# Experts of 64 tokens or fewer get slots, weight buffers and a short branch of their own between the turns of the others

## Chip, cores and metric

The kernel runs on one core of a Trainium2 chip. The metric is the device time of one execution in microseconds (us); lower is better. The program is one launch that does the whole computation.

## The reference

Three layers follow one another: gated linear attention, a dense layer with three-way maximum, and a mixture of eight experts of which each token uses one. The change touches the last layer only:

```python
N, D, E, F = (3072, 384, 8, 1024)          # tokens, model width, experts, hidden width
logits = x @ w_gate
e_idx = np.argmax(logits, axis=1)
...
for e in range(E):
    mask = e_idx == e
    if not mask.any():
        continue
    h = np.maximum(x[mask] @ w1[e], 0.0)
    ye = h @ w2[e]
    out[mask] = gate_w[mask, None] * eom[mask, e, None] * ye
```

Everything is float32. How many tokens go to which expert depends on the data. For the inputs of this kernel the routing gives experts 0 to 7 these numbers of tokens: 4, 281, 1078, 7, 47, 262, 107 and 1286. So three experts (0, 3 and 4) have 64 tokens or fewer.

## The kernel before

**Stages.** Attention and the dense layer run over eight blocks of 384 tokens. While the last block is finished, the expert layer starts. From then on the core works through *units*: a unit is up to 256 tokens of one expert (or up to 320 in the last unit of an expert, so that a rest of 64 or fewer rides along). The unit list is computed on the chip from the routing (`units_a_ops` to `units_e`, L730 to L835, all on VectorE): which expert each unit has, whether its expert is new (`meta`), and its kind (`kinds`). The kinds are 0 (two tiles of 128 tokens), 1 (an expert with 64 tokens or fewer, "alone"), 2 (two tiles and a third of 64) and 3 (one tile). Here there are 15 units: 0 to 4 are expert 7, 5 is expert 0 (alone), 6 is expert 1 (kind 2), 7 to 10 expert 2 (the last of kind 2), 11 and 12 experts 3 and 4 (alone), 13 expert 5 (kind 2), 14 expert 6 (kind 3). Units 0 and 1 run within the end of the dense layer; units 2 to 14 are the *turns* of the function `turn` (L1279), unrolled in the program. From unit 10 on, a turn lies within an If on the number of units.

**One turn** of unit u, in program order: registers and token gathers for unit u+2 (GpSimd, indirect DMA, L857); the first four pieces of the second weight matrix are split into a high and a low float32r part if the expert is new (`fresh`, `split2`, ScalarE and VectorE, L644 and L645); `up` (L918: for each of eight slices of the hidden layer 15 matmuls, then one ScalarE and one or two VectorE evictions out of one of three PSUM banks, L919 and L922); the other four pieces; the load of the first weight matrix of unit u+2; `tx` (transposes of the gathered tokens of unit u+1, L880, and their split) and `split1` of unit u+1 if it is new; `down` (L961 and L966/L967, one PSUM bank for each tile, evicted by ScalarE into a fresh output tile, L973, and scattered to HBM by GpSimd, L938); the load of the second weight matrix of unit u+2. Each engine runs its instructions in this order, and waits only where its next instruction needs something.

**Weights.** Each expert has 1.57 MB in each of two matrices. They are loaded into the raw buffers `s1` and `s2`, two of each, by the parity of the unit (`stage`, L847, on SP's queue, two units ahead). Kinds 0, 2 and 3 split them into `w1H`, `w1L`, `w2H`, `w2L`; kind 1 multiplies with the raw float32 buffers.

**An alone unit** runs through the same turn with short arms: `tx` copies the transposed tokens to `xF` (L891), `up` has six float32 products of 64 tokens in pairs over the two halves of the array (L909, 12 instructions in the trace) and one ScalarE copy to `hF` (L932), `down` transposes the hidden values (L985), applies the maximum with zero (L988, L990), has eight float32 products (L909, 16 instructions) and adds the two halves up (`put_sum`, L948 to L950). Only the experts' own numbers decide which arm a turn takes: `by_kind` (L895) is a chain of Ifs on a register.

**The list before the turns.** The steps that end the dense layer and start the experts are written out by hand (`then`, L1215 on): `units_b` makes the slot of each token and two big products for the index lists (`mark`, L668 to L670), `up_some(1, ...)` is the up stage of unit 1, `units_c` looks the indices up (`lookup`), then `units_d`, `units_e`, and the gathers of units 2 and 3.

## Time and profile before

| what | value |
|---|---|
| median of 3 runs | 763.56 us (763.53 to 764.07) |
| profiled execution, device time | 759.59 us |
| its span, first to last instruction | 757.8 us |
| TensorE matmuls busy | 705.9 us (93% of the span) |
| VectorE, ScalarE, GpSimd busy | 52%, 38%, 17% |
| mean granted TensorE clock | 0.978 of 2.4 GHz |

Times are counted from the span's start. "Idle before" is time in which an engine did nothing before an instruction, and the arrow says what ended it: another engine's instruction, a DMA, or "issue" where the profile shows nothing that it waited for. PEld is TensorE's weight load, which runs beside the matmuls; a name with a q behind it (PEldq, ACTq) is an engine's sequencer with its branches and register loads. A granted clock of 1.00 is 2.4 GHz, 0.5 is 1.2 GHz.

### The profile page before, as it was taken

The page shows a single profiled execution, that of the slowest core. Times are in us where ns is not written, and L with a number is a line of the kernel's source. Part 1 is how long each engine was busy: PE and PEld are TensorE (multiplying, and loading weights), DVE is VectorE, ACT ScalarE, POOL GpSimd, SP SyncE. Part 2 cuts the span into 40 slices and gives each one's busy share as a digit, 9 for nine tenths or more (in the row PEclk, how much of TensorE's full clock was granted, in tenths as well). Part 3 has the DMA queues.
Part 4 walks back from the last instruction along what each step waited for, and adds up shares of the span by engine and source line. Part 5 has one row for each costly group of instructions (what it writes and reads, how often), then busy time and mean ns, then how long its engine had stood idle before and what let it go on. Part 6 is the DMA issues. An engine that isn't in the chain of part 4 may idle for free. (4 is left out here: it accounts for less than half of the span.)

```text
span 757.8 us, 14282 instructions
## 1 busy us (share of the span) xinstructions
PE 705.9 (93%) x5056; PEld 656.3 (87%) x5056; DVE 397.7 (52%) x929; ACT 288.5 (38%) x752; POOL 126.8 (17%) x136
## 2 busy tenths in 40 slices
PE   8999999999899999999999999999989999977980
PEld 8989999798799999999999999999949899954970
DVE  7968976477957547364143566532237422213640
ACT  4455344454444424335131243332236423224540
POOL 1000000011121202111111130422232322231220
PEclk9999999999999999999999999999989999997995
DMA  9823400651412215000000060214553113666310
GB/s 265 340 57 137 144 1 22 181 134 45 124 51 73 69 40 131 15 24 5 22 19 10 22 229 22 62 58 138 208 214 112 52 51 132 204 237 218 99 43 17
DMA packets 23407, 76.33 MB, mean 101 GB/s; under 512 B 8026, under 2 KB 12132, under 8 KB 20208
## 3 DMA queue, kind: packets, MB, share of 16 engines
q1 hardware_dynamic: 17424, 60.95, 24.6%
q0 software_dynamic: 4704, 12.91, 5.4%
q8 instruction: 67, 1.10, 0.6%
q10 hardware_dynamic: 1152, 0.89, 0.4%
q14 instruction: 60, 0.49, 0.2%
HBM read 89.26 MB, written 9.94 MB: 131 GB/s over the span
## 5 line engine op out<-in xcount | busy, mean ns | idle before, releaser
L918 PE MATMUL psM<-cx,w1H 128*128 128x256 f32 (+1 forms) x576 | 112.1, 292 | 5.3 <-DVE ch L922 4.9
L482 POOL TENSOR_TENSOR hL<-hm,hH 128x384 fp32r<-128x384 f32 x36 | 42.2, 1172 | 396.6 <-ACT hH L477 396.6
L456 PE MATMUL hps<-xH,wH 128*128 128x384 f32 x432 | 103.9, 347 | 1.4 <-ACT xH L367 1.3
L456 PE MATMUL hps<-xH,wL 128*128 128x384 f32 x432 | 98.4, 335 | 1.6 <-DVE wL L425 1.6
L918 PEld LDWEIGHTS psM<-cx,w1H 128*128 128x128 f32 x576 | 91.3, 188 | 8.8 <-DVE ch L922 4.3
L456 PE MATMUL hps<-xL,wH 128*128 128x384 f32 x432 | 98.6, 335 | 0.0
L961 PE MATMUL psP<-w2H,ch 128*128 128x384 f32 x368 | 96.8, 338 | 1.1 <-ACT w2H L644 1.1
L922 DVE SCALAR_TENSOR_TENSOR ch<-psM,ch 128x256 fp32r<-128x256 f32 (+1 forms) x128 | 43.9, 371 | 95.2 <-ACT ch L919 92.1
L918 PE MATMUL psM<-cx,w1L 128*128 128x256 f32 (+1 forms) x288 | 83.6, 290 | 0.0
L456 PEld LDWEIGHTS hps<-xH,wH 128*128 128x128 f32 x432 | 74.1, 188 | 7.4 <-ACT xH L367 2.1
L456 PEld LDWEIGHTS hps<-xH,wL 128*128 128x128 f32 x432 | 76.9, 188 | 2.3 <-DVE wL L425 2.3
L456 PEld LDWEIGHTS hps<-xL,wH 128*128 128x128 f32 x432 | 77.3, 188 | 0.2 <-DVE xL L368 0.2
L492 PE MATMUL ops<-wo,hH 128*128 128x400 f32 x258 | 68.5, 346 | 0.2
L961 PEld LDWEIGHTS psP<-w2H,ch 128*128 128x128 f32 x368 | 66.6, 188 | 2.0 <-issue 1.3
L463 DVE TENSOR_TENSOR hm<-hm,hps 128x384 f32<-128x384 f32 x48 | 26.4, 551 | 69.7 <-PE hps L456 62.7
L919 ACT ACTIVATE ch<-psM 128x256 fp32r<-128x256 f32 (+1 forms) x96 | 37.7, 402 | 64.8 <-PE psM L918 55.4
L938 POOL DMA_INDIRECT out<-yo,sidx x30 | 31.1, 1038 | 185.8 <-ACT yo L973 147.8
L961 PE MATMUL psP<-w2L,ch 128*128 128x384 f32 x184 | 61.5, 334 | 0.0
L857 POOL DMA_INDIRECT xg<-x2d,gidx x49 | 50.4, 1029 | 30.1 <-PE psM L918 12.2
L918 PEld LDWEIGHTS psM<-cx,w1L 128*128 128x128 f32 x288 | 54.2, 188 | 0.0
L477 ACT CAST hH<-hm 128x384 fp32r<-128x384 f32 x43 | 22.0, 513 | 81.0 <-DVE hm L466 77.2
L492 PEld LDWEIGHTS ops<-wo,hH 128*128 128x128 f32 x258 | 47.0, 188 | 1.3 <-ACT hH L477 0.5
(238 smaller groups left out, 1111.5 us busy)
## 6 DMA issues: line engine op xcount, KB each, us to landing
s1a<-in_ew SPq DMA_DIRECT2D x9, 1536.0 KB
s2a<-in_ew SPq DMA_DIRECT2D x9, 1536.0 KB
s1b<-in_ew SPq DMA_DIRECT2D x7, 1536.0 KB
s2b<-in_ew SPq DMA_DIRECT2D x7, 1536.0 KB
ws<-in_w SPq DMA_DIRECT2D x6, 1152.0 KB
at<-in_al SPq DMA_DIRECT2D x16, 336.9 KB
vt<-in_v SPq DMA_DIRECT2D x8, 576.0 KB
x2d<-xs SPq DMA_DIRECT2D x24, 192.0 KB
```

What stands on the lines that cost most here:

```text
L456: mm(ps, slab(a, f)[:, w, k], b[i][:, k], start=(n == 0), stop=(n == 8))
L463: nc.vector.tensor_max(m, m, ps)
L477: nc.scalar.copy(hH[i, f], m)
L482: (nc.gpsimd if not general and i > 1 else nc.vector).tensor_sub(hL[i, f], hps["m"], hH[i, f].bitcast(F32))
L492: mm(ps[:, :DM + NG], a[i, f][:, ts_], wo[f // 3][:, b, f % 3], start=(f + n == 0), stop=(f + n == 7))
L857: nc.gpsimd.indirect_dma_start(out=xg[u % 2, t][:p], out_offset=None, in_=x2d[:n, :], in_offset=bass.IndirectOffsetOnAxis(ap=gidx[:p, 3 * ...
L918: mm(ps, w[:, k, f * 128:(f + 1) * 128], x[:, k, :n], start=(k + m == 0), stop=(k + m == 4))
L919: nc.scalar.activation(chid(0, f, slice(0, n)), ps, AF.Relu)
L922: nc.vector.scalar_tensor_tensor(C["h"][f // 4][:, f % 4, to:to + b - a], ps[:, a:b], 0.0, chid(0, f, slice(a, b)).bitcast(F32), op0=ALU.m ...
L938: nc.gpsimd.indirect_dma_start(out=out[:, :], out_offset=bass.IndirectOffsetOnAxis(ap=sidx[:p, c:c + 1], axis=0), in_=y[:p], in_offset=Non ...
L961: mm(ps[:, :DM], chid(x, f, slice(128 * t, 128 * t + 128)), w[:, f], start=(f + n == 0), stop=(f == NE - 1 and n == 2))
```

## The change

An expert with a rest of 64 tokens or fewer and nothing else no longer gets a unit (`nu` subtracts `few`). It gets one of eight slots behind the unit slots in the index lists (62 instead of 54 columns), computed in `units_a_ops` and `units_b`, and the new `units_f` writes a list of these experts and their number to `tiny`. Kind 1 and its arms go.

Each of the turns 2 to 9 (i = 0 to 7) now has, behind `down`, an If on the number of such experts (`n_own > i`) with the function `own(i)`: the float32 arm of before, with its up products in two halves of 256 columns. Its tokens are gathered by `gather_own` into `xO`, transposed and copied to `xF` within the `tx` of the same turn (`own=True`: these three transposes run in all eight turns, whether there is such an expert or not). With the data above, `own` runs in turns 2, 3 and 4, all of expert 7, and the unit list has 12 entries: 0 to 4 expert 7, 5 expert 1, 6 to 9 expert 2, 10 expert 5, 11 expert 6.

The second pair of raw weight buffers now belongs to `own` (`stage_own`, loaded as soon as the one before is done); the units share one pair, so `stage(u + 1, 0)` comes at the start of turn u and `stage(u + 1, 1)` behind the pieces of `split2`. Of these pieces two instead of four come ahead of `up`. The output tiles are three fixed buffers, cleared once on GpSimd, and the scatters (`put`) come last in a turn, behind `own`, `gather_own` and, from unit 9 on, inside the arms of the If that holds the next turn. `put2` scatters units 0 and 1.

```diff
--- before.py
+++ after.py
-NS = 3 * (NU - NF)
+NS = 3 * (NU - NF) + NE
...
     def split2(j, pieces=range(NE)):
         for f in pieces:
-            split(*(t[:, f] for t in (C["s2"][j % 2], *C["w2"])))
+            split(*(t[:, f] for t in (C["s2"][0], *C["w2"])))
...
         nu = wt([128, NE], "nsl")
-        nc.vector.scalar_tensor_tensor(nu, q, 1.0, f, op0=ALU.add, op1=ALU.subtract)
+        nc.vector.scalar_tensor_tensor(nu, q, 1.0, few, op0=ALU.add, op1=ALU.subtract)
...
+
+        own = rtmp["own"] = wt([128, NE], "own")
+        nc.vector.tensor_sub(own, few, f)
+        yield
+        nth = rtmp["nth"] = wt([128, NE], "nth")
+        nc.vector.tensor_tensor_scan(nth, one8, own, 0.0, ALU.mult, ALU.add)
+        yield
         over = rtmp["over"] = q
         nc.vector.tensor_scalar(over, q, 3.0, 1.0, op0=ALU.mult, op1=ALU.add)
         yield
-        nc.vector.tensor_mul(over, over, f)
+        off = rtmp["off"] = wt([128, NE], "off")
+        nc.vector.tensor_sub(off, nth, over)
+        yield
+        nc.vector.tensor_sub(off, off, base)
+        yield
+        nc.vector.scalar_tensor_tensor(off, off, 3.0 * NU, own, op0=ALU.add, op1=ALU.mult)
+        yield
+        nc.vector.tensor_sub(off, off, f)
+        yield
+        nc.vector.tensor_mul(over, over, few)
         yield
...
     def units_b():
         bt = wt([128, NT, NE], "bt", BF16)
         sums = []
-        for n, name in (("over", "so"), ("base", "sl")):
+        for n, name in (("over", "so"), ("off", "sd"), ("base", "sl")):
             nc.vector.tensor_tensor(bt, oh, rtmp[n].unsqueeze(1).to_broadcast([128, NT, NE]), ALU.mult)
             sums.append(wt([128, NT], name))
             nc.vector.tensor_reduce(sums[-1], bt, op=ALU.add, axis=AX.X)
-        so, sl = sums
+        so, sd, sl = sums
         nc.vector.scalar_tensor_tensor(so, rdiv, 1.0, so, op0=ALU.add, op1=ALU.is_equal)
+        nc.vector.tensor_mul(so, so, sd)
         nc.vector.tensor_add(sl, sl, rdiv)
-        nc.vector.tensor_sub(sl, sl, so)
+        nc.vector.tensor_add(sl, sl, so)
         rtmp["q"] = mark(sl, ioS, NT)
...
-        nc.vector.tensor_copy(kinds[:, :NU], kd)
-
-        nc.vector.scalar_tensor_tensor(kinds[:, 2 * NU:], kd, 1.0, meta[:, NU:2 * NU], op0=ALU.is_equal, op1=ALU.max)
-        nc.vector.scalar_tensor_tensor(kinds[:, NU:2 * NU], kd, 1.0, meta[:, NU:2 * NU], op0=ALU.not_equal, op1=ALU.mult)
+        nc.vector.tensor_copy(kinds, kd)
+
+    def units_f():
+
+        own, nth = rtmp["own"], rtmp["nth"]
+        nc.vector.tensor_mul(own, own, nth)
+        wide = [128, NE, NE]
+        le = wt(wide, "bt")
+        nc.vector.tensor_tensor(le, own.unsqueeze(1).to_broadcast(wide), ioU[:, 1:NE + 1].unsqueeze(2).to_broadcast(wide),
+                                ALU.is_equal)
+        nc.vector.tensor_tensor(le, le, ioU[:, :NE].unsqueeze(1).to_broadcast(wide), ALU.mult)
+        ex = wt([128, NE], "fv")
+        nc.vector.tensor_reduce(ex, le, op=ALU.add, axis=AX.X)
+        nc.vector.tensor_copy(tiny[:, :NE], ex)
+        nc.vector.tensor_copy(tiny[:, NE:], nth[:, NE - 1:])
...
-        chg[u] = nc.values_load(kinds[0:1, 2 * NU + u:2 * NU + u + 1], engines=(ET.SP,), min_val=0, max_val=1)
+        chg[u] = nc.values_load(meta[0:1, NU + u:NU + u + 1], engines=(ET.SP, ET.Activation, ET.DVE), min_val=0, max_val=1)
-        new[u] = nc.values_load(kinds[0:1, NU + u:NU + u + 1], engines=(ET.Activation, ET.DVE),
-                                min_val=0, max_val=1)
+
+    def load(e, buf, n, cond):
+        s, w = (("s1", ew1), ("s2", ew2))[n]
+        nc.sync.dma_start(out=C[s][buf], in_=w[ds(e, 1)].rearrange("o p a b -> p (o a) b"), cond=cond)
 
     def stage(u, n):
-        s, w = (("s1", ew1), ("s2", ew2))[n]
-        nc.sync.dma_start(out=C[s][u % 2], in_=w[ds(eos[u], 1)].rearrange("o p a b -> p (o a) b"), cond=(chg[u] == 1))
+        load(eos[u], 0, n, chg[u] == 1)
+
+    def stage_own(i, both=range(2)):
+        if i < NE:
+            e = nc.values_load(tiny[0:1, i:i + 1], engines=(ET.SP,), min_val=0, max_val=NE - 1)
+            for n in both:
+                load(e, 1, n, n_own > i)
 
...
+    def take(x, p, c, n=NTOK):
+        nc.gpsimd.indirect_dma_start(out=x[:p], out_offset=None, in_=x2d[:n, :],
+                                     in_offset=bass.IndirectOffsetOnAxis(ap=gidx[:p, c:c + 1], axis=0),
+                                     bounds_check=n - 1, oob_is_err=False)
...
+    def gather_own(i):
+        if i < NE:
+            take(C["xO"], LAST, 3 * NU + i)
 
 
     def hidden():
+        C["y"] = [bp.tile([128, DM], F32, tag="hL", name="yo", bufs=7) for _ in range(3)]
+        for y in C["y"]:
+            nc.gpsimd.memset(y, 0.0)
...
-        def alone():
-            nc.scalar.copy(C["xF"], ps[0][:, :DM])
-
-        by_kind(u, {1: alone}, whole)
+                nc.tensor.transpose(ps[t][:, k * p:k * p + p], x[:p, k * 128:(k + 1) * 128], ident[:p, :p])
+        if own:
+            x = C["xO"]
+            nc.vector.tensor_copy(C["gO"], x[:LAST, DM:XW])
+            for k in range(3):
+                nc.tensor.transpose(ps[2][:, (3 + k) * LAST:(4 + k) * LAST], x[:LAST, k * 128:(k + 1) * 128], ident[:LAST, :LAST])
+        for t in range(tiles):
+            p = WIDTH[t]
+            x = ps[t][:, :3 * p].rearrange("p (k c) -> p k c", k=3)
+            h = hi[:, :, 128 * t:128 * t + p]
+            nc.scalar.copy(h, x)
+            nc.vector.tensor_sub(lo[:, :, 128 * t:128 * t + p], x, h.bitcast(F32))
+        if own:
+            nc.scalar.copy(C["xF"], ps[2][:, 3 * LAST:6 * LAST])
...
     def up(u):
-        def alone():
-            ps = bank(psM, "M", "psM1")
-            w = C["s1"][u % 2]
...
-
-        by_kind(u, {1: alone, 2: lambda: up_some(u, 256 + LAST, range(NE))}, lambda: up_some(u, 256, range(NE)))
-
-    def put(u, t, y, p):
-        c = 3 * u + t
+        by_kind(u, {2: lambda: up_some(u, 256 + LAST, range(NE))}, lambda: up_some(u, 256, range(NE)))
...
+    def send(y, p, c):
...
+    def put(u):
+        def some(*ts):
+            for t in ts:
+                send(C["y"][t], WIDTH[t], 3 * u + t)
+
+        some(0)
+        by_kind(u, {2: lambda: some(1, 2), 3: lambda: None}, lambda: some(1))
+
...
         if t == 2:
-            return put_sum(u, t, ps)
-        y = out_tile()
-        nc.scalar.activation(y, ps[:, :DM], AF.Copy, scale=gate[u % 2][:, t:t + 1])
-        if not general:
-            put(u, t, y, 128)
-        return y
+            return sum_up(C["y"][t], gate[u % 2][:64, t:t + 1], ps)
+        nc.scalar.activation(C["y"][t], ps[:, :DM], AF.Copy, scale=gate[u % 2][:, t:t + 1])
 
     def down(u):
-        def alone():
...
-        def tiles(n):
-            return lambda: [down_tile(u, t) for t in range(n)]
-
-        by_kind(u, {1: alone, 2: tiles(3), 3: tiles(1)}, tiles(2))
+        down_tile(u, 0)
+        by_kind(u, {2: lambda: [down_tile(u, t) for t in (1, 2)], 3: lambda: None}, lambda: down_tile(u, 1))
+
+
+
+    def own(i):
+        h, w = C["hF"], C["s1"][1]
+        for a in range(0, 512, 256):
+            ps = bank(psM, "M", "psM1")
+            for k in range(3):
+                x = C["xF"][:, k * LAST:(k + 1) * LAST]
+                halves(ps, 256, (x, x), [w[:, k, g * 512 + a:g * 512 + a + 256] for g in range(2)], k == 0, k == 2)
+            nc.scalar.copy(h[:, a:a + 256], ps[:, :256])
...
+        ps = bank(psO, "O", "psP")
+        w = C["s2"][1]
+        for f in range(4):
+            x = h[:, 512 + f * 128:512 + (f + 1) * 128]
+            halves(ps, DM, (x[:, :64], x[:, 64:]), (w[:, f], w[:, f + 4]), f == 0, f == 3)
+        sum_up(C["yO"], C["gO"], ps)
+        send(C["yO"], LAST, 3 * NU + i)
...
+    def put2(u):
+        for t in range(2):
+            send(C["y"][t], 128, 3 * u + t)
...
+    then(put2, 0)
     then(units_b)
...
     then(units_e)
+    then(units_f)
     then(gather, NF + 1)
...
-    for u in (NF, NF + 1):
-        load_meta(u)
-        for n in range(2):
-            stage(u, n)
-    C["xF"] = bp.tile([128, DM], F32, tag="hH", name="xF", bufs=7)
+    C["xO"], C["gO"] = bp.tile([128, XW], F32, tag="x32", name="xO"), wk.tile([LAST, 1], F32, name="gO")
+    C["xF"] = bp.tile([128, 3 * LAST], F32, tag="hH", name="xF", bufs=7)
     C["hF"] = bp.tile([128, FF2], F32, tag="x32", name="hF")
+    C["yO"] = bp.tile([128, DM], F32, tag="hH", name="yO", bufs=7)
     n_all = nc.values_load(meta[0:1, 2 * NU:2 * NU + 1], min_val=0, max_val=NU)
+    n_own = nc.values_load(tiny[0:1, NE:NE + 1], min_val=0, max_val=NE)
+    load_meta(NF)
+    for n in range(2):
+        stage(NF, n)
+    stage_own(0)
...
     def fresh(u, split, *a):
-        with tc.If(new[u] == 1):
+        with tc.If(chg[u] == 1):
...
+    gather_own(0)
     tx(NF)
...
     def turn(u):
         more = u + 1 < NU
-        ahead = u + 2 < NU
-        if ahead:
+        i = u - NF
+        if more:
+            stage(u + 1, 0)
+        if u + 2 < NU:
             load_meta(u + 2)
             gather(u + 2)
-        fresh(u, split2, low)
+        fresh(u, split2, range(2))
         up(u)
-        fresh(u, split2, high)
-        if ahead:
-            stage(u + 2, 0)
+        fresh(u, split2, range(2, NE))
         if more:
+            stage(u + 1, 1)
             with guard(u + 1):
-                tx(u + 1)
+                tx(u + 1, own=i < NE)
                 fresh(u + 1, split1)
         down(u)
-        if ahead:
-            stage(u + 2, 1)
-        if more and u + 1 >= NV:
-            with guard(u + 1):
+        if i < NE:
+            with tc.If(n_own > i):
+                own(i)
+            stage_own(i + 1)
+            gather_own(i + 1)
+        if u + 1 < NV:
+            put(u)
+        elif more:
+            with tc.If(n_all > u + 1) as c:
+                put(u)
                 turn(u + 1)
-
+            with c.Else():
+                put(u)
+        else:
+            put(u)
...
+    put2(1)
 
     for u in range(NF, NV):
         turn(u)
```

## Rows read from the trace of the kernel before

**Rows 1.** Busy time of each engine by window, one window for each turn; the last is the tail.

```profile
core 0: us, PE busy (x) PEld busy (x) DVE busy (x) ACT busy (x) POOL busy (x), PEclk, DMA share, GB/s
...
553.65:567.34 13.69, 9.93 (x43) 3.79 (x42) 6.11 (x14) 6.11 (x13) 4.92 (x4) 0.76 0.74 279
567.34:591.34 24.00, 23.29 (x148) 22.49 (x146) 13.60 (x37) 13.01 (x29) 6.65 (x6) 1.00 0.29 98
...
611.36:629.41 18.05, 18.05 (x130) 17.81 (x130) 4.95 (x14) 5.33 (x13) 5.04 (x5) 1.00 0.17 52
...
647.43:670.37 22.94, 22.94 (x146) 22.12 (x145) 4.72 (x19) 5.72 (x12) 6.05 (x6) 1.00 0.54 182
670.37:683.14 12.77, 7.37 (x42) 3.18 (x42) 2.07 (x7) 3.55 (x7) 4.86 (x5) 1.00 0.94 345
683.14:697.97 14.83, 11.41 (x41) 4.66 (x41) 5.53 (x12) 5.06 (x11) 2.96 (x3) 0.65 0.59 216
697.97:722.49 24.52, 23.36 (x147) 22.26 (x146) 13.69 (x37) 13.27 (x30) 6.26 (x6) 1.00 0.33 104
722.49:738.12 15.63, 13.42 (x96) 12.72 (x96) 7.64 (x17) 7.14 (x18) 3.94 (x4) 1.00 0.19 42
738.12:757.80 19.68, 0.00 (x1) 0.00 (x0) 0.00 (x0) 0.58 (x1) 1.03 (x1) 0.59 0.07 17
```

**Rows 2.** Timeline of TensorE in turns 11 and 12 (start, us, what, idle before).

```profile
670.37 2.79 PE L909 MATMUL psM<-s1b,xF 128*64 128x512 f32 x12
...
674.87 0.63 PE L985 MATMUL psH<-ident,hF 128*128 128x128 f32 x4 [0.56 <-ACTq L1272]
...
675.84 2.80 PE L909 MATMUL psP<-s2b,hF 128*64 128x384 f32 x16 [0.34 <-ACT hF L990]
683.14 4.49 PE L909 MATMUL psM<-s1a,xF 128*64 128x512 f32 x12 [4.50 <-issue]
```

**Rows 3.** Timeline of TensorE in turn 5.

```profile
559.17 0.67 PE L985 MATMUL psH<-ident,hF 128*128 128x128 f32 x4 [1.58 <-ACT w1H L644]
562.02 5.39 PE L909 MATMUL psP<-s2b,hF 128*64 128x384 f32 x16 [2.17 <-ACT hF L990]
```

**Rows 4.** Timeline of TensorE in the up stages of turns 7 and 14.

```profile
596.42 0.51 PE L918 MATMUL psM<-cx,w1H 128*128 128x256 f32 x2 [1.73 <-DVE ch L922]
...
726.99 0.51 PE L918 MATMUL psM<-cx,w1H 128*128 128x256 f32 x2 [1.07 <-DVE ch L922]
```

**Rows 5.** Timeline of VectorE at the start of turn 7.

```profile
594.00 2.03 DVE L645 TENSOR_TENSOR w2L<-s2b,w2H 128x384 fp32r<-128x384 f32 x4 [0.56 <-ACT w2H L644]
```

**Rows 6.** Timeline of VectorE from `units_a_ops` to the first eviction of unit 1.

```profile
470.62 0.17 DVE L770 TENSOR_TENSOR fv<-base,first 128x8 f32<-128x8 f32 x1
470.82 0.17 DVE L772 TENSOR_TENSOR base<-base,fv 128x8 f32<-128x8 f32 x1
...
471.87 0.35 DVE L786 TENSOR_TENSOR bt<-oh,q 128x192 bf16<-128x192 bf16 x1
...
472.64 0.36 DVE L786 TENSOR_TENSOR bt<-oh,base 128x192 bf16<-128x192 bf16 x1
...
473.86 1.51 DVE L668 TENSOR_TENSOR eq<-sl,ioS 128x1296 bf16<-128x1296 f32 x1
475.40 1.51 DVE L670 TENSOR_TENSOR q<-eq,tno 128x1296 bf16<-128x1296 bf16 x1
477.08 1.32 DVE L922 SCALAR_TENSOR_TENSOR ch<-psM,ch 128x256 fp32r<-128x256 f32 x3 [0.17 <-ACT ch L919]
```

**Rows 7.** Timeline of TensorE around the same place and before the first turn.

```profile
477.19 0.28 PE L918 MATMUL psM<-cx,w1L 128*128 128x256 f32 x1
477.56 0.51 PE L918 MATMUL psM<-cx,w1H 128*128 128x256 f32 x2
...
491.36 0.52 PE L880 MATMUL psT<-ident,xg 128*128 128x128 f32 x3 [0.73 <-issue]
```

**Rows 8.** The tile `xg`: time of a token gather from issue to landing.

```profile
DMA to landing us min/median/max: 2.7/3.7/8.4
```

**Rows 9.** Source line L899 (`by_kind`): TensorE's branches, ns min/median/max.

```profile
L899 PEldq COMPARE_BRANCH  x83: 63/210/5753, 491.5 to 735.5; - x83
```

**Rows 10.** Source line L840 (the kind of a unit): TensorE's register loads.

```profile
L840 PEldq TENSOR_LOAD <-kinds x15: 298/303/540, 488.8 to 719.4; - x15
```

More of the change, by code (lines that the diff above doesn't have):

```diff
@@ L879, in tx @@
             for k in range(3):
-                nc.tensor.transpose(ps[t][:, k * 128:k * 128 + p], x[:p, k * 128:(k + 1) * 128], ident[:p, :p])
-        def whole():
-            for t in range(tiles):
-                p = WIDTH[t]
-                x = ps[t][:, :DM].rearrange("p (k c) -> p k c", k=3)[:, :, :p]
-                h = hi[:, :, 128 * t:128 * t + p]
-                nc.scalar.copy(h, x)
-                nc.vector.tensor_sub(lo[:, :, 128 * t:128 * t + p], x, h.bitcast(F32))
-        def alone():
-            nc.scalar.copy(C["xF"], ps[0][:, :DM])
-        by_kind(u, {1: alone}, whole)
+                nc.tensor.transpose(ps[t][:, k * p:k * p + p], x[:p, k * 128:(k + 1) * 128], ident[:p, :p])
[12 more added lines that the diff above has]
+            nc.scalar.copy(C["xF"], ps[2][:, 3 * LAST:6 * LAST])
     def by_kind(u, arms, rest):
@@ new lines, in down_tile @@
+            return sum_up(C["y"][t], gate[u % 2][:64, t:t + 1], ps)
+        nc.scalar.activation(C["y"][t], ps[:, :DM], AF.Copy, scale=gate[u % 2][:, t:t + 1])
+    def down(u):
+        down_tile(u, 0)
[8 more added lines that the diff above has]
+            nc.scalar.copy(h[:, a:a + 256], ps[:, :256])
+        for a in range(0, 512, 256):
+            ps = bank(C["psH"], "H", "psH")
+            for f in range(2):
+                nc.tensor.transpose(ps[:, f * 128:(f + 1) * 128], h[:, a + f * 128:a + (f + 1) * 128], ident)
+            hs = h[:, 512 + a:768 + a]
+            if a:
+                nc.vector.tensor_scalar_max(hs, ps[:, :256], 0.0)
+            else:
+                nc.scalar.activation(hs, ps[:, :256], AF.Relu)
+        ps = bank(psO, "O", "psP")
[5 more added lines that the diff above has]
+        send(C["yO"], LAST, 3 * NU + i)
```

87 lines of the change are left out of this document (33 added, 54 removed).

## Prediction

> **What bounds the kernel now.** I read the busy shares first, then the turns by window, then TensorE's own timeline for its idle times, and last what stands ahead of each idle time. TensorE bounds the turns: in a plain turn it is busy for the whole of 18.05 us, in a turn of kind 2 for 22.94 us, while VectorE, ScalarE and GpSimd are busy 4 to 7 us in each [rows 1]. So what takes TensorE's time, or lets it idle, is paid in full, and the rest is hidden. Three turns are different: the alone turns 5, 11 and 12 take 13.69, 12.77 and 14.83 us, in which TensorE is busy for only 9.93, 7.37 and 11.41, partly at half clock (granted 0.76 and 0.65 of 2.4 GHz) [rows 1]. The reader should see in them one short arm at full clock, in turn 11: 2.79 us of up products, 0.63 of transposes, 2.80 of down products, with idle times of 0.56 and 0.34 [rows 2]; and three ways to lose time. In turn 5 the arm's copies queue on ScalarE behind the next expert's split: 1.58 and 2.17 idle, then 5.39 for the same 16 products as 2.80, which is the 1.2 GHz level [rows 3]. Behind turn 11 TensorE waits 4.50 us for nothing that the profile shows, and then needs 4.49 instead of 2.79 [rows 2]. And the turns that follow pay too: turns 6 and 13, of kind 2 with a new expert, take 24.00 and 24.52 instead of 22.94 [rows 1].
>
> The 4.50 us lie where the sequencer jumps from one short arm over the long ones; TensorE's branches in these Ifs take 0.21 us in the median and 5.75 at most [rows 9]. The DMA engines are 94% busy in that window [rows 1], so a fetch of code would be slow.
>
> **What goes.** Turns 5, 11 and 12 as a whole: 13.69 + 12.77 + 14.83 = 41.29 us. The excess of turns 6 and 13 over 22.94: 1.06 + 1.58 = 2.64, as these follow a dense turn in future. In turns 7 and 14 the up stage stops for 1.73 and 1.07 us since VectorE evicts the first hidden slice only after four split pieces [rows 4], which take 2.03 [rows 5]. With two pieces ahead of it that work starts 1.0 earlier; three PSUM banks carry the matmuls a little further, and I leave 0.25 us in each: 1.73 + 1.07 - 0.50 = 2.30. Together 46.23 us.
>
> **What comes on TensorE.** Three runs of `own`. The busy time of turn 11's arm, 2.79 + 0.63 + 2.80 = 6.22, is the lower bound. With turn 5's idle times, 6.22 + 1.58 + 2.17 = 9.97 is the upper. The new arm stands behind `down`, so the next expert's split has long left ScalarE, and its first 256 columns are copied while the second 256 are multiplied; what is left is the copy, transpose and maximum of the second half, as in turn 11. I take 6.22 + 0.56 + 0.34 = 7.1 us, times 3 = 21.3. The three transposes of 64 tokens in eight `tx`: four of 128 tokens take 0.63 [rows 2], so three take 0.47 at most and half of it at least; I take 0.4, times 8 = 3.2.
>
> **What comes on VectorE ahead of the turns.** Here its list is on the path. TensorE's up stage of unit 1 stands from 477.19 to 477.56 for the bank that VectorE frees with the eviction of 477.08, and that eviction comes right behind the second index product [rows 6, 7]. So each microsecond more in `units_a_ops` to `mark` is one more on TensorE. The added work: five small dependent operations at 0.2 (470.62 to 470.82) = 1.0 [rows 6]; one more product and sum over all tokens, 471.87 to 472.64 = 0.77, and a product at 0.2; the two index products 62/54 as long, 2 x 1.51 x 8/54 = 0.45. Sum 2.4. Behind that, `units_f` is six more operations for two fewer in `units_e`, and TensorE now loads `n_own` from their result ahead of its other registers: 0.73 idle at 491.36 today [rows 7], about 0.8 more for four operations net and 0.3 for the load [rows 10]. I take 2.4 + 1.1 = 3.5, with 1.0 as the lower bound (if other waits absorb the chain) and 5.2 as the upper (if TensorE falls to half clock over it, priced by the extra 1.70 of 4.49 against 2.79 [rows 2]).
>
> **What is moved.** The scatters and the gather of the next small expert come later on GpSimd, behind the scatter of `own`. GpSimd is busy 5 to 7 us of a turn [rows 1], so three or four issues more fit, and the fixed output tiles are needed again only near the end of the next turn. But the next `tx` waits for `xO` in TensorE's own order. That gather leaves some microseconds into a turn, while the loads for `own` (3.1 MB) are still running, and has to land within half of it. A gather lands in 2.7 to 8.4 us [rows 8]; the spread of 5.7 is the bound, nothing the other, and as the half turn of 9 us is longer than the slowest landing I take 0.5 in all.
>
> The unit weights have one buffer pair now. `s2` of the next expert can start when the six late pieces are split, about 6 x 0.51 = 3.0 us [rows 5] into the second half of a turn of 22.94, which leaves 11.5 - 3.0 = 8.4 us. A load of 1.57 MB takes 4.6 us at the 345 GB/s of turn 11 and 7.3 at the 216 of turn 12 [rows 1]. It fits by 1 to 4 us, in both places where a new expert follows a new one (turns 5 to 6 and 10 to 11), so I cost it at nothing; without that room each microsecond late is one of TensorE's. `s1` has from the turn's start to the up stage's end and is nearer to fitting still. The clearing of the output tiles falls where GpSimd has nothing to do. The tail after the last matmul, 19.68 us [rows 1], I leave as it is: the last scatter still follows ScalarE's last eviction.
>
> **Sum.** -46.23 + 21.3 + 3.2 + 3.5 + 0.5 = -17.7 us. The profiled execution took 759.59 (span 757.8 and 1.8 around it), so it would take 741.9; the median of the runs shown lies 0.5% above the profiled one, and 763.56 x 741.9 / 759.59 = 745.8. The favourable bounds, 46.23 - 18.7 - 1.9 - 1.0 = 24.6, give 739; the others without a change of clock in `own` (9.97 x 3 + 3.8 + 5.2 + 5.7 = 44.6) give nearly no gain, but not all at once.
>
> **Rivals.**
> 1. *`own` at half clock.* After idle times of 1.6 to 4.5 us the arm's products took 5.39 for 2.80 and 4.49 for 2.79 [rows 2, 3]. If gaps around `own` do the same, one run costs 2.59 + 1.70 + about 0.4 more = 4.7; one of three gives 750.5, all three 760. Against it: in turn 11 the clock stayed at 1.00 through idle times of 0.56 and 0.34 [rows 1, 2], and `own` is nearest to that. 12%.
> 2. *Loads late.* With one pair, and two queues sharing the engines, a load at half the rates above takes 9.2 to 14.6 us, 1 to 6 late at each of two places: 747 to 758. 8%.
> 3. *The new Ifs stop TensorE: slower.* Eight tests of `n_own` are added in the turns. If each costs the 4.50 us that turn 12 waited [rows 2], that is 36 us: 782. It decides from 17.7 / 8 = 2.2 us for a test. For it: the branch of 5.75 us; against it the median of 0.21 over 83 branches, [rows 9], and that plain turns, whose up Ifs jump over a longer arm than `own`, have no idle time at all [rows 1]. 6%.
> 4. *More gain*: `own` near its busy time and the VectorE chain partly absorbed: 739 to 742. 4%.
> 5. *Nothing moves*, by several of the costs together or since no expert is that small: the trace has three alone turns [rows 1], so the second is excluded. 2%.
>
> The Trainium skill, "Runtime: NRT & Kernel Launch", section "Instruction fetch mechanics", says that a taken branch to code outside the small prefetched part has to wait for a DMA that brings it, since prefetch only goes straight on. By that rule the skipped `own` arms of turns 5 to 9 are five such places, and the sum would be rival 3's with its condition; the trace agrees with it at the 4.50 us of turn 12 and shows no cost for the jump in plain turns, so I keep the sum.
>
> **How the numbers follow.** The forecast holds 68%, and 740 to 751 is its own range. To leave out no more than 2 in 10 the range takes in the favourable end and most of rivals 1 and 2: 739 to 755. The measurement tells 0.2% (1.5 us) from no change. Faster: the forecast, rival 4, rival 2 and nearly all of rival 1 give 0.91; slower is rival 3 with 0.06; the rest is 0.03.
>
> **What would show it.** Right: ten turns instead of thirteen; three windows some 7 us longer than 18.05 or 22.94, each with 24 + 16 products of L909's function at full clock; a stop of some 2.5 us in unit 1's up stage near 477 us; the up stops in the turns with a new expert near 0.25; no wait for weights at turns 6 and 11. Wrong: idle times named issue at the test of `n_own`; products of `own` at twice the length; transposes or VectorE waiting for `xO`; splits waiting for `s2`. If the gain is much over 25 us, I have mis-sized the VectorE chain or the tail.

## The result, and the profile after

The changed kernel takes 747.01 us (median of 4 runs, 744.44 to 747.87), the kernel before 763.82 beside it (4 runs, 763.53 to 765.11): a ratio of 0.9771, 95% interval 0.9744 to 0.9799. The forecast was 745.8, its range 739 to 755. The profiled execution took 744.44 with a span of 742.7, so 15.1 us of span went, and they went otherwise than the sum had it:

| stretch | before | after | change | forecast |
|---|---|---|---|---|
| span's start to the first turn | 494.67 | 498.18 | +3.5 | +3.5 |
| the turns | 243.45 | 231.78 | -11.7 | -21.2 |
| last matmul to the end | 19.68 | 12.74 | -6.9 | 0 |

The turns by window, one row each, the last row the tail (columns as in [rows 1]):

```profile
498.18:523.30 25.12, 24.81 (x177) 20.94 (x176) 5.15 (x16) 7.12 (x18) 4.00 (x4) 1.00 0.51 188
523.30:548.46 25.16, 24.75 (x178) 20.87 (x176) 5.89 (x17) 7.80 (x19) 6.95 (x7) 1.00 0.46 169
548.46:578.26 29.80, 29.64 (x195) 25.54 (x193) 11.27 (x32) 12.31 (x27) 7.89 (x7) 1.00 0.61 217
578.26:603.60 25.34, 23.57 (x151) 22.48 (x149) 14.21 (x39) 14.47 (x32) 10.86 (x10) 1.00 0.49 175
603.60:623.97 20.37, 18.37 (x132) 17.84 (x133) 8.78 (x24) 8.92 (x22) 8.25 (x8) 1.00 0.19 60
623.97:645.70 21.73, 19.95 (x133) 19.42 (x133) 5.01 (x15) 5.63 (x14) 5.77 (x7) 0.92 0.16 48
645.70:665.87 20.17, 18.43 (x132) 17.90 (x133) 4.97 (x15) 5.64 (x14) 5.95 (x7) 1.00 0.17 52
665.87:690.87 25.00, 23.31 (x149) 22.45 (x149) 10.16 (x30) 10.13 (x22) 4.59 (x5) 1.00 0.63 226
690.87:714.10 23.23, 23.20 (x146) 22.32 (x146) 13.33 (x37) 12.05 (x27) 6.90 (x6) 1.00 0.35 113
714.10:729.96 15.86, 13.20 (x97) 12.28 (x96) 7.62 (x17) 7.41 (x18) 5.25 (x5) 1.00 0.18 47
729.96:742.70 12.74, 0.00 (x0) 0.00 (x0) 0.00 (x0) 0.58 (x1) 1.02 (x1) 0.67 0.11 28
```

There are ten turns in place of thirteen. Turns 2 to 4 run `own` and are 7.1, 7.1 and 6.9 us longer than 18.05 and 22.94 [rows 1], with TensorE busy nearly throughout. Turns 5 to 9 should be plain or of kind 2 again, and the reader sees that they are not: each is some 2 us too long (turn 7 3.7), and TensorE's busy time falls short of the window by 1.7 to 2.0. The tail is 7 us shorter than the one of [rows 1].

TensorE's timeline, first its stops ahead of the turns, then `own` in turn 2, then the stops in the turns:

```profile
479.93 0.50 PE L965 MATMUL psM<-cx,w1H 128*128 128x256 f32 x2 [2.40 <-DVE ch L969]
494.87 0.52 PE L930 MATMUL psT<-ident,xg 128*128 128x128 f32 x3 [1.83 <-issue]
...
516.92 2.81 PE L956 MATMUL psM<-s1b,xF 128*64 128x256 f32 x24
519.66 0.98 PE L1032 MATMUL psH<-ident,hF 128*128 128x128 f32 x4
520.57 2.80 PE L956 MATMUL psP<-s2b,hF 128*64 128x384 f32 x16
...
603.60 0.47 PE L965 MATMUL psM<-cx,w1H 128*128 128x256 f32 x2 [1.63 <-issue]
...
623.97 0.47 PE L965 MATMUL psM<-cx,w1H 128*128 128x256 f32 x2 [2.00 <-issue]
...
645.70 0.47 PE L965 MATMUL psM<-cx,w1H 128*128 128x256 f32 x2 [1.78 <-ACTq L1352]
...
665.87 0.53 PE L965 MATMUL psM<-cx,w1H 128*128 128x320 f32 x2 [1.74 <-ACTq L1352]
...
690.87 0.53 PE L965 MATMUL psM<-cx,w1H 128*128 128x320 f32 x2 [1.69 <-ACTq L1352]
...
718.42 0.51 PE L965 MATMUL psM<-cx,w1H 128*128 128x256 f32 x2 [1.10 <-DVE ch L969]
...
725.37 0.41 PE L1002 MATMUL psP<-w2H,ch 128*128 128x384 f32 x1 [1.56 <-PEq L1347]
```

`own` takes 6.4 us (516.92 to 523.30), its products at full clock. Five stops of 1.63 to 2.00 us, 8.84 in all, stand at the starts of the five turns that follow a skipped `own` (L1352 is its If). A microsecond after the 2.00 the granted clock falls to 1.2 GHz for 3.4 us, which makes turn 7 1.5 us longer than turn 8 (21.73 against 20.17 us, less 0.04 for their stops).

The sequencer's records show what lies in such a stop. TensorE, between turns 6 and 7 (start and end in us; matmuls' ends are modelled):

```
618.71 618.92 COMPARE_BRANCH  L1352   the jump over own's arm
621.63 621.97 MATMUL          L1002   last one of the down stage
622.01 622.07 EVENT_SEMAPHORE L1352   the If's balancing event
622.16 622.74 COMPARE_BRANCH  L949    two, in put
622.80 623.43 TENSOR_LOAD ... L875    kind of the unit after next, to a register
623.49 623.81 COMPARE_BRANCH  L949    up's kind
623.87 623.92 EVENT_SEMAPHORE L965    ahead of the first weight load
623.97        MATMUL          L965    first one of turn 7
```

The jump itself takes 0.21 us and lies under the matmuls. The event of the skipped path ("balancing": it raises the semaphores that the arm would have raised) comes 0.04 us after the last matmul's end in all five places, and the semaphore that it waits for in its record is the one that TensorE's own matmuls raise. So it waits for the array to empty; all control work behind it is then uncovered. Where `own` runs, there is no such event: the same branches and the register load (521.18 to 522.87) lie under `own`'s last matmuls, 0.4 to 2.1 us ahead of the next turn's first (523.30), and nothing stops.

**Theory A**: the stop is that wait (drain), and its price is the control work between the event and the next matmul. **Theory B**: it is the jump over the arm's code, priced by its length. A third reading (handshake in the expectations) is that TensorE waits for ScalarE's event of the same If, which the profile names at three of the five stops (ACTq L1352). In the records that event ends 0.4 to 1.2 us ahead of TensorE's first weight load in all five places (622.77 against 623.94 in the one above), so it does not set these stops. The stop of 1.56 us in turn 11 stands behind another skipped If, the one around `tx`; the kernel before had 1.13 at that place. For the tail: GpSimd's scatter now stands inside the last arm, so that its jump into the arm can be done while it waits for the last tile.

### The profile page after: what moved, and what is told of

The parts are those of the page before. It is cut to its first block, busy times and chain, and to the rows that moved or that the text cites. A ratio compares the mean times of both kernels' runs of the same rounds, so it can differ in the third digit from the quotient of the medians.

```text
span 742.7 us, 14157 instructions
## 1 busy us (share of the span) xinstructions
PE 699.4 (94%) x5089; PEld 655.4 (88%) x5089; DVE 399.9 (54%) x943; ACT 290.4 (39%) x760; POOL 128.2 (17%) x138
## 5 line engine op out<-in xcount | busy, mean ns | idle before, releaser
L965 PE MATMUL psM<-cx,w1H 128*128 128x256 f32 (+1 forms) x576 | 112.8, 294 | 13.6 <-ACTq L1352 5.2
L965 PEld LDWEIGHTS psM<-cx,w1H 128*128 128x128 f32 x576 | 91.7, 190 | 18.3 <-issue 6.4
L965 PE MATMUL psM<-cx,w1L 128*128 128x256 f32 (+1 forms) x288 | 83.9, 291 | 0.0
L965 PEld LDWEIGHTS psM<-cx,w1L 128*128 128x128 f32 x288 | 55.1, 191 | 0.0
L976 POOL DMA_INDIRECT out<-yo,sidx x27 | 29.4, 1088 | 117.2 <-ACT yo L1013 48.0
L894 POOL DMA_INDIRECT xg<-x2d,gidx x40 | 41.7, 1042 | 24.9 <-issue 13.4
```

What stands on the lines that cost most here:

```text
L894: nc.gpsimd.indirect_dma_start(out=x[:p], out_offset=None, in_=x2d[:n, :], in_offset=bass.IndirectOffsetOnAxis(ap=gidx[:p, c:c + 1], axis= ...
L965: mm(ps, w[:, k, f * 128:(f + 1) * 128], x[:, k, :n], start=(k + m == 0), stop=(k + m == 4))
L976: nc.gpsimd.indirect_dma_start(out=out[:, :], out_offset=bass.IndirectOffsetOnAxis(ap=sidx[:p, c:c + 1], axis=0), in_=y[:p], in_offset=Non ...
```

## The experiments

All start from the changed kernel, e7 to e11 with the edits of e6 in it, and ran with this data, which has three experts for `own`. The third plain turn is turn 8, which is 18.0 us where nothing stops. "From unit 1" is the time from the first matmul of unit 1's up stage to the span's end, since what lies ahead of it differs by up to 4.3 us between the runs. It still holds a stretch at half clock ahead of the turns, of 3.4 us in e1 to e3, e5 to e7 and e10 and of 6.8 us in e8 and e9, which after, e4 and e11 do not have there; e8 has another of 3.4 us in turn 5.

| run | median, us | ratio (95%) | turn 8 | from unit 1 | tail |
|---|---|---|---|---|---|
| after | 747.01 | 0.9771 (0.9744 to 0.9799) | 20.17 | 268.5 | 12.8 |
| e1 three slots | 736.55 | 0.9646 (0.962 to 0.9672) | 17.99 | 259.8 | 12.4 |
| e2 registers early | 740.0 | 0.9695 (0.9672 to 0.9718) | 19.09 | 262.9 | 12.8 |
| e3 test inside tile 0 | 741.37 | 0.9708 (0.9685 to 0.9732) | 18.59 | 263.7 | 12.8 |
| e4 put ahead of the If | 751.24 | 0.9839 (0.9816 to 0.9862) | 19.87 | 273.7 | 18.6 |
| e5 short arms | 745.38 | 0.9758 (0.9725 to 0.979) | 19.69 | 268.0 | 13.1 |
| e6 = e2 and e3 | 739.9 | 0.968 (0.965 to 0.9709) | 18.59 | 262.0 | 12.8 |
| e7 one skip | 741.35 | 0.9711 (0.9678 to 0.9745) | 17.99 | 262.9 | 12.6 |
| e8 one skip, front | 744.87 | 0.9759 (0.9724 to 0.9794) | 17.99 | 265.8 | 12.7 |
| e9 three slots, any routing | 737.27 | 0.9661 (0.9634 to 0.9688) | 17.99 | 260.2 | 12.5 |
| e10 arm lengths | 744.18 | 0.9741 (0.971 to 0.9773) | 18.59 | 266.9 | 16.2 |
| e11 = e9, front | 734.23 | 0.9595 (0.9568 to 0.9622) | 17.99 | 254.9 | 12.5 |

**e1. Three slots in place of eight** (an own expert beyond the third would be left out; this data has none).

```diff
+NO = 3
...
-        if i < NE:
+        if i < NO:
             with tc.If(n_own > i):
                 own(i)
```

> Only the three slots that this data fills are kept: no test of n_own, no gather, no transposes of xO in turns 5 to 9. In the changed kernel TensorE is idle 1.63, 2.00, 1.78, 1.74 and 1.69 us behind the five skipped arms, 8.84 in all, and the clock fell once, in turn 7, for about 1.6 us. If the skipped arms are the price, all of this goes, with 5 x 0.2 of transposes: 735.5 to 738.5 instead of 747.0. If the idle times belong to the turn change itself (any turn would show them once its predecessor is as dense), they stay, and only the 1.0 of transposes goes: 746.

All five stops are gone and turn 8 is 17.99 us. The median is 10.5 us below the changed kernel's. The 8.84, the half clock behind one of them (1.5) and five transposes of an unused `xO` (0.19 a turn) make 11.3; a stop of 1.04 that now shows in turn 6's up stage takes some of it back. So the skipped tests cost the kernel about that much.

**e2. Registers loaded ahead of the down stage.**

```diff
-            load_meta(u + 2)          # at the turn's start
...
+        if u + 2 < NU:
+            load_meta(u + 2)
         down(u)
```

> The register loads for unit u+2 stand ahead of down instead of at the turn's start; nothing else moves. Theory drain: behind a skipped arm TensorE's sequencer can go on only when the array has finished, and the control work up to the next matmul (branches, one register load with two companions of 0.75 us together, the branch of up) is no longer hidden. Then each of the five idle times falls by 0.7 to 0.8: 743.3, idle about 1.0 each. Theory handshake (TensorE waits until ScalarE has evicted the last tile and passed the same If) and theory code fetch (the jump itself): idle times stay at 1.6 to 2.0 and the time at 747.

The stops are 1.20, 1.31, 1.10, 0.96 and 1.20 us, 5.77 in all, 0.61 less each: about what stands between 622.80 and 623.43 above. In two of the five (turns 6 and 10) the handshake now sets the end: TensorE's last record ends at 605.05 and 687.32, its weight load waits for the end of ScalarE's event at 605.37 and 687.67. The median is 3.3 below the forecast 743.3. The gain beyond the stops is the missing half clock, the stop of 1.10 at 718.42, of which 0.33 is left, and up stages that are 0.2 to 0.3 us shorter in turns 6 to 8, which the edit does not explain. Why the stop at 718.42 goes, VectorE's timeline in turn 11 shows; after:

```profile
715.51 0.61 DVE L992 SCALAR_TENSOR_TENSOR yo<-ylo,gate,yo 64x384 f32<-64x384 f32 x1 [4.15 <-issue]
717.01 1.03 DVE L646 TENSOR_TENSOR w2L<-s2a,w2H 128x384 fp32r<-128x384 f32 x2 [0.89 <-ACT w2H L645]
717.95 1.08 DVE L969 SCALAR_TENSOR_TENSOR ch<-psM,ch 128x256 fp32r<-128x256 f32 x3
```

and with the registers early:

```profile
712.10 0.61 DVE L992 SCALAR_TENSOR_TENSOR yo<-ylo,gate,yo 64x384 f32<-64x384 f32 x1 [4.15 <-issue]
712.83 1.03 DVE L646 TENSOR_TENSOR w2L<-s2a,w2H 128x384 fp32r<-128x384 f32 x2
```

VectorE and ScalarE loaded two registers each between the sum and the split; without them the split follows at once.

**e3. The own test between the halves of the down stage's first tile** (and `own`'s sums in another PSUM bank).

```diff
-        down(u)
+        down_tile(u, 0, low)
         if i < NE:
             with tc.If(n_own > i):
                 own(i)
+        down_tile(u, 0, high)
+        down(u)               # without tile 0
```

> The test of n_own and own stand between the two halves of the first down tile, where no branch and no register load follows on TensorE; own's sums use the transposes' PSUM bank. Theory drain: a skipped arm costs the drain, one branch and a weight load, 0.2 to 0.5 instead of 1.77: 738.5 to 740.5 with the clock dip gone. Theory handshake: ScalarE reaches the If only after the copies of tx and, in turn 5, the late split pieces, so 0.5 to 3 stay: 741 to 746. Theory code fetch: the jump is as long as before, 747.

No stop of 1 us is left at a skip: the event still comes 0.04 us after the last matmul's end, and the next matmul 0.11 behind it. Turn 8 is 18.59 us. The median, 741.37, is 0.9 above the range given for drain and inside the handshake's; the records decide for drain. The stop in turn 11 stays (1.10), as it should without e2's edit, and one of the same kind shows in turn 6, where the changed kernel has none:

```profile
609.10 0.50 PE L965 MATMUL psM<-cx,w1H 128*128 128x256 f32 x2 [1.12 <-DVE ch L969]
```

**e4. The scatters ahead of the If.**

```diff
+        put(u)
         if u + 1 < NV:
-            put(u)
...
             with tc.If(n_all > u + 1) as c:
-                put(u)
                 turn(u + 1)
-            with c.Else():
-                put(u)
```

> The scatters of units 9 and later stand ahead of the If of the next turn instead of in its arms; all else as in the changed kernel. Its tail after the last matmul was 12.74 us against 19.68 before. Theory arms: with the scatters in both arms GpSimd leaves the If chain without waiting for TensorE's far jump, and its drain of 6.4 us starts early; then the old tail comes back: 752 to 754, tail 18 to 20. Rival: the tail is shorter because the chain of Ifs is shorter (12 units instead of 15) and the code that is jumped over nearer: 747, tail 12 to 13.

The tail is 18.6 us, 5.8 longer; the span is 6.7 longer, the median 4.2, a little less than the 5 to 7 forecast. GpSimd's records at the end:

```
                       put in the arm (after)   put ahead (e4)
branch of the last If  722.31                   735.40
next record            726.36, in the arm       739.21, behind the If
scatter's issue        730.90                   731.76
two INC_SWDGE_SEM      730.93 to 734.70         731.77 to 735.22
a third                                         739.63 to 741.37
DRAIN                  735.43 to 741.87         742.09 to 748.53
```

In the kernel before the same branch lies at 742.75 and its next record at 747.50, the third INC_SWDGE_SEM ends at 749.67, the drain runs from 750.29 to 756.89. With the scatter inside the arm, GpSimd has jumped into it by 726.36, 3.6 us ahead of the last matmul's end, while it waits for the last tile: it comes to the drain 4.5 us after the scatter, not 10.3 (e4) or 11.2 (before). That the 3.8 us behind the branch at 735.40 are the jump is read from the gap alone; the branch's own record lasts 0.05.

**e5. Short arms where none runs.**

```diff
-                own(i)
+                own(i) if i < 3 else own_head()   # own_head: first product group and its copy
```

> The own arms of turns 5 to 9, which this data never enters, hold one product group and one copy (12 matmuls) in place of the whole short branch (some 58 TensorE instructions); the first three arms stay whole. Theory A (the stop at a skipped arm is TensorE's balancing event, which waits until the array has emptied, and the branches and register loads that then lie open): the length of the arm does not matter, the five idle times stay at 1.6 to 2.0 us each, 8.5 to 9 us in all, and the time is 746 to 748 us. Theory B (the stop is the jump over the arm's code, priced by its length): the five stops fall under 1 us each and the time is 741 to 743.5 us.

The stops are 1.52, 1.78, 1.68, 1.53 and 1.49 us, 8.0 in all where theory A had 8.5 to 9: each 0.1 to 0.2 shorter, none near 1. The median is 0.6 below the range of theory A, and its runs (741.94 to 747.69) overlap those of the changed kernel (744.44 to 747.87). Theory B falls for arms of this length. Of the 0.8 us, 0.6 lie between the last branch and the first matmul, where e5 has no event of L965 (623.87 above); why not is open.

**e6. Both remedies, e2 and e3.**

> Both remedies together: the test of the own arm stands between the halves of the down stage's first tile, and the registers of turn u+2 are loaded ahead of the down stage of turn u. Theory A: a skipped arm costs its own event and branch alone, about 0.4 us inside the down stage and nothing that is seen at the turn's start; the stop of 1.10 us in turn 11's up stage, which the two register loads on VectorE made, is gone as in the run with early registers; the span of 738.1 us falls by 1.5 to 2 and the time is 737.5 to 739.5 us. Theory B: no better than either remedy alone, 740 to 741.5 us.

The event still comes 0.04 us after the last matmul's end in all five places, but the next matmul starts 0.15 us after that end, since no branch and no register load stands between. Turn 8, by windows, and beside it that of e1:

```profile
646.02:664.61 18.59, 18.44 (x133) 17.91 (x133) 4.93 (x15) 5.66 (x14) 6.01 (x6) 1.00 0.40 123
```

```profile
643.55:661.54 17.99, 17.99 (x131) 17.75 (x130) 4.78 (x14) 5.22 (x13) 5.04 (x5) 1.00 0.41 139
```

So 2.18 us for a skip in turn 8 (20.17 against 17.99) part into 1.08 with e2's edit (0.78 of it the shorter stop), 0.50 for the other control work (e6) and 0.60 that stay with the If and the unused `xO`. The median, 739.9, is 0.4 above the range given and no better than e2's: from unit 1 the gain over e2 is 0.9 us, and in the profiled runs unit 1 began 1.4 us later than in e2. What keeps the gain so small is the arm that is entered. Turns 5 to 9 take 103.7 us against 106.8 in e2, but turns 2 to 4 take 82.3 against 80.0: `own` now follows `tx` so closely that TensorE waits in it for ScalarE's copies of `xF` and `hF`, where after and e2 have no stop over 0.16.

```profile
540.61 2.81 PE L956 MATMUL psM<-s1b,xF 128*64 128x256 f32 x24 [0.81 <-ACTq L1325]
568.14 2.81 PE L956 MATMUL psM<-s1b,xF 128*64 128x256 f32 x24 [0.52 <-ACT xF L943]
571.52 0.71 PE L1031 MATMUL psH<-ident,hF 128*128 128x128 f32 x4 [0.58 <-ACT hF L1027]
```

The copy of `xF` ends at 540.56, so the first of these waits for it too.

**e7. Slots 4 to 7 inside the arm of slot 3**, each with its own loads, gather and transposes: one skip in place of five.

```diff
             with tc.If(n_own > i):
                 own(i)
+                if i == NO:           # NO = 3
+                    more_own(i + 1)   # If n_own > 4: loads, gather, tx_own, own(4), and so on
```

> As the run with both remedies, but the own arms of slots 4 to 7 stand inside the arm of slot 3 (turn 5), each with its loads, its gather and its transposes: every routing is still computed, and with this data one arm is skipped in place of five. Theory A: four skips less at 0.4 us each, and TensorE does not transpose an unused xO in turns 5 to 8 (0.2 us each): 2 to 2.5 us below the run with both remedies, 735 to 737 us. If the cost of a skip inside the tile is already hidden, no change within 0.5 us.

A miss: 741.35, where 735 to 737 was expected. Turns 6 to 9 are free of skips (one stop of 0.42 is left in turn 6), but the one skip that is left stops TensorE longer than before:

```profile
600.37 0.41 PE L1006 MATMUL psP<-w2H,ch 128*128 128x384 f32 x1 [2.19 <-PEq L1367]
```

Its jump is in the sequencer's records from 596.82 to 600.20, 3.38 us, where in after and e2 to e6 a jump over one `own` took 0.21 to 0.43, once 0.79. So theory B is not dead; it needs a long arm. The longer stop takes back 2.0 of the 2.9 us that turns 6 to 9 gain over e6; turns 2 to 4 are 0.55 longer than in e6 and turn 10 0.9, which was not followed up.

**e8. As e7, and two slices of unit 1 ahead of the VectorE chain.**

```diff
+    then(up_some, 1, 256, range(2))
     then(units_b)
-    then(up_some, 1, 256, range(NE - 2))
+    then(up_some, 1, 256, range(2, NE - 2))
```

> As the run with one skip, and the first two slices of the second fixed unit's up stage stand ahead of the longer VectorE chain (the sums for slots, base and offset). If the chain is what stops TensorE for 2.40 us at 479.93, as the prediction's step has it: the stop goes, the chain ends 0.7 to 1.5 us later, which the stop before the turns (1.83 us) may take back in part; 1 to 2.4 us below the run with one skip, 733 to 735.5 us. If the first turn is held by the end of the chain itself (lookup, gather, registers), nothing is gained, and the stop moves from 479.93 to the start of the turns.

Nothing was gained, as the rival had it, but the stop did not move to the turns (1.74 there): it grew to 4.69 us.

```profile
488.07 0.80 PE L969 MATMUL psM<-cx,w1H 128*128 128x256 f32 x2 [4.69 <-DVE ch L973]
```

`units_b` runs under the down stage of unit 0. Behind two evictions VectorE waits 2.95 us until TensorE comes to those slices, so the whole chain ends later, and the slices behind it wait for all of it.

**e9. Three slots for any routing**, on e6: the planner counts an expert of 64 tokens or fewer beyond the third as an ordinary unit.

```diff
+        nc.vector.scalar_tensor_tensor(own, nth, NO + 0.5, own, op0=ALU.is_lt, op1=ALU.mult)
+        nc.vector.tensor_add(few, f, own)      # ahead of the number of units
```

> The run with both remedies, with three own slots in place of eight; the planner gives a fourth or later expert of 64 tokens or fewer an ordinary unit, so that every routing is computed (two more VectorE operations in the planner's chain, one of them behind another, some 0.3 us). Theory: no arm is skipped with this data, so five tests at about 0.4 us and five unused transposes of xO at 0.2 us fall away against the run with both remedies, less 0.3: measured from the same stop in front (2.40 us) to the end of the span 253 to 254.5 us where that run has 256.2; the median 736 to 738.5 us. Rival: the skips inside the tile were hidden and only the transposes fall away: 255.3 us and 738.5 to 739.5.

The median is in the range, 2.6 us below e6. From the end of the stop in front it is 253.9 us, as forecast for skips that are not hidden, against 256.2 in e6. The stop itself is 2.99 instead of 2.40, and the clock is at half for 6.8 us around its end, as the window from unit 1's up stage to the first turn shows (PEclk 0.88):

```profile
475.40:502.75 27.35, 22.52 (x154) 21.70 (x154) 15.50 (x56) 6.53 (x14) 8.98 (x9) 0.88 0.18 55
```

**e10. Own arms 1, 2, 3, 4 and 5 times as long**, in slots 3 to 7, none of which runs, on e6.

```diff
-                own(i)
+                for _ in range(max(1, i - 2)):
+                    own(i)
```

> The run with both remedies, with the own arms of slots 3 to 7, never entered with this data, holding the short branch 1, 2, 3, 4 and 5 times over. It asks what the jump over an arm costs TensorE's sequencer by the arm's length: 0.22 us over one body and 3.38 us over five (nested) in the runs before. Theory L (by length): about 0.8 us more for each body, so jumps of 0.2, 1.0, 1.8, 2.6 and 3.4 us; the sequencer runs ahead of the array by some 1.2 us at that place, so stops of 0.4, 0.4, 0.6, 1.4 and 2.2 us, and a time some 3 us above the run with both remedies, 742 to 744 us. Theory F (one step: code already at hand or not): 0.2 to 0.4 us up to some length and 3 to 3.5 us from there on; where the step lies at two bodies four stops of 2.2 us, 746 to 748 us.

The jumps take 0.22, 0.35, 0.33, 0.33 and 3.70 us: a step between four and five bodies, no slope. Four skips stop TensorE for 0.15 us, the fifth, in turn 9, for

```profile
679.40 0.41 PE L1002 MATMUL psP<-w2H,ch 128*128 128x384 f32 x1 [1.66 <-PEq L1352]
```

as some 2 us of its jump (675.52 to 679.23) lie under the matmuls. Theory F held in kind; it guessed the step at two bodies, and its time (746 to 748) was too high. The tail is 16.2 us, 3.4 more than in e6. GpSimd's records place it at the last If of the program, on a flag that is not set: its next record comes 3.5 us after the branch there (731.47 to 734.97), where after and e6 have 0.4. No run was made on its cause.

**e11. As e9, with three slices between the last two long operations of the chain.**

```diff
-    then(up_some, 1, 256, range(NE - 2))
+    then(up_some, 1, 256, range(3))
+    then(lambda: rtmp["held"].pop()())   # ScalarE's scaling and VectorE's product of the index marks
+    then(up_some, 1, 256, range(3, NE - 2))
```

> The run with three slots for any routing, and the fixed unit's first three slices of the up stage stand between the two long operations at the end of the planner's sums (the comparison 128x1488 of 1.71 us ahead of them; ScalarE's scaling and VectorE's product, 1.71 us, behind them). Theory: the stop of 2.40 us at the fourth slice shrinks to 0.5 us, since VectorE evicts three slices (1.09 us) 1.8 us earlier, and the lookup, which TensorE comes to after the sixth slice, does not wait for the later product: 1.5 to 2 us below the run with three slots, 734 to 736.5 us. Rival, as in the run in which two slices stood ahead of the whole chain: the chain's end is what holds, and the stop comes back at the lookup: no gain, 736 to 738.5 us.

It is the fastest, 734.23 us (730.63 to 735.01). Like e9 it is written for every routing; only this one was run. The stop is 1.02 us, not the 0.5 expected. TensorE's and VectorE's timelines there:

```profile
482.73 0.50 PE L977 MATMUL psM<-cx,w1H 128*128 128x256 f32 x2 [1.02 <-DVE ch L981]
```

```profile
480.63 1.71 DVE L670 TENSOR_TENSOR eq<-sl,ioS 128x1488 bf16<-128x1488 f32 x1
482.26 1.08 DVE L981 SCALAR_TENSOR_TENSOR ch<-psM,ch 128x256 fp32r<-128x256 f32 x3
483.26 1.70 DVE L674 TENSOR_TENSOR q<-eq,tno 128x1488 bf16<-128x1488 bf16 x1
```

The three evictions come ahead of the second long operation. The clock stayed at its full level, as the same window shows (it did in after, too, behind 2.40 us):

```profile
478.37:501.07 22.70, 19.85 (x154) 19.07 (x154) 15.22 (x56) 6.86 (x14) 8.96 (x9) 1.00 0.22 66
```

Against e9's 27.35 us that is 4.65 less, about 2 for the stop and the rest for the clock.

## Why the prediction was right, and where it was not

The time was right by luck: the cost of the skipped tests, left at nothing, was offset by a tail and an `own` that were priced too dear. The mechanism of each term is seen in the trace.

- **VectorE's chain** (3.5 us): right. The stop ahead of unit 1's fourth slice is 2.40, as the added operations gave, and the one before the turns rose from 0.73 [rows 7] to 1.83, by 1.1. e8 and e11 move it as the step says: the chain, evictions and TensorE's slices are one line of waits.
- **`own` and the transposes**: right in kind, too dear. The forecast was 7.1 and 0.4 each; `own` takes 6.4, as the copies' idle times are at most 0.16, and the transposes 0.19, just under their lower bound. Turns 2 to 4 are 21.0 us longer than 18.05 and 22.94, where 22.5 was forecast: 1.5 too dear.
- **The skipped tests**: the step that failed. The prediction gave the If itself no cost and let rival 3 decide at 2.2 us for each of eight tests. Three tests enter their arm and stop nothing; five skip it and cost 1.77 on average, 8.84 in all, with 1.5 more for the half clock in turn 7. The row on which I leaned, plain turns without idle time at their up Ifs, shows Ifs with a matmul stream in either arm; the event that waits for the last matmul stands in these traces only where the path taken holds none of TensorE's work. The trace of the kernel before had one such place, which the prediction did not use: the If around `tx` that its last turn skips. Its event comes at 732.62, 0.04 us after the last matmul's end, three branches follow until 733.55, and the stop is 1.13:

```profile
733.72 0.41 PE L961 MATMUL psP<-w2H,ch 128*128 128x384 f32 x1 [1.13 <-ACT w2H L644]
```

- **The tail**: left at 19.68, it is 12.74. I looked at what the last scatter waits for, not at what GpSimd has still to do behind it. e4 shows that the place of the scatter decides: 18.6 with it ahead of the If.
- **The up stops of turns with a new expert**: wrong in both turns. In turn 11 1.10 stayed for the 0.25 forecast. Turn 6 shows none only because the skip's 1.63 stands ahead of it: e1 and e3, without that stop, have 1.04 and 1.12 there. Two split pieces stand ahead of the eviction as assumed, but two register loads stand ahead of these, which `load_meta` had put there; with the loads moved, e6 has 0.34 in either turn.
- **Sum over the turns**: 8.84 for the skips, 1.5 for the clock and 0.85 for turn 11's up stop, 0.43 for its skipped `tx` (1.56 against 1.13), less 1.5 for `own` in turns 2 to 4 and 0.5 for waits on `xO` that did not occur, make 9.6; the gap between -21.2 and -11.7 is 9.5. It is offset by the tail's -6.9. The rest, 2.6 us, is what the profiled execution, 744.44, lies above the 741.9 forecast for it; between the medians it is 1.2 (747.01 against 745.8).
- **Rivals**: `own` at half clock and late loads did not occur: full clock in turns 2 to 4, no stop from turn 5 to turn 11 that names a load. Rival 3's mechanism was there at 1.77 us for five of eight tests, under its point of decision.

The Trainium skill, "Runtime: NRT & Kernel Launch", section "Instruction fetch mechanics", says that a taken branch to code outside a small prefetched part waits for that code. The runs agree for a long arm only: 3.3 to 3.7 us over five bodies, 0.2 to 0.4 (once 0.79) over one to four. It does not explain the stops of the changed kernel, which e5 leaves and e2 and e6 shorten without touching the arm.

## What to carry to other kernels

An If that holds TensorE's work on one path only can cost more when it is skipped than when it is entered: place it where matmuls follow at once, with no branch or register load between, but not so near to what makes the arm's inputs that the entered arm waits (e6), and test no more often than the data can need. At the end of a program ask what each engine does behind its last useful instruction; a scatter inside the last arm lets GpSimd jump while it waits. When a chain on VectorE stops TensorE, put evictions between its long operations, not ahead of it.

## What the runs showed of the hardware

- The balancing event of a skipped `own` lies 0.04 us behind the end of the last matmul in all 34 places where the jump was short (five each in after and e2 to e6, four in e10); in e7, e8 and e10's fifth it follows the late jump. At the skipped `tx` of turn 11 it lies 0.4 to 1.5 us behind the modelled end of the last matmul in after and the experiments, 0.04 in before; why is open.
- A jump of TensorE's sequencer over code has a step: 0.22 to 0.35 us in e10 over up to four short branches of 44 matmuls and as many weight loads, 3.33 to 3.70 over five (e7, e8, e10).
- Stops of 1.8 to 3 us are followed by a stretch at 1.2 GHz in some places and not in others: 3.4 us in turn 7 of the changed kernel (granted 0.92 in its window) and not behind its other four; 3.4 us behind e1's 2.40 and none behind the changed kernel's; 6.8 us at e9's 2.99. One such stretch of 3.4 us costs about 1.5.
- GpSimd's drain at the end takes 6.4 to 6.6 us in each of before, after and e4, and each INC_SWDGE_SEM between the last scatter and it 1.7.
